# Casts on VectorE, k evacuation on ScalarE and hand-made instruction orders in an attention and spectral-mix kernel

## The chip, the cores and the metric

The kernel runs on one core of a Trainium2 chip. The metric is the device time of one execution, in microseconds (us). An execution more than 1.5% above the fastest of its kernel counts as slow and is left out of the ratios. TensorE, VectorE, ScalarE and GpSimd are the compute engines; the profile calls them PE, DVE, ACT and POOL. PEld is TensorE's weight load. In this kernel TensorE's products go into tiles in PSUM, and nearly all else lies in tiles in SBUF. To evacuate is to copy a product out of PSUM. The granted clock is the share of TensorE's full clock that it was given.

## The reference, cut to what matters

```python
# q, k, v: (8, 8, 576, 64) float32; window 128, causal, ALiBi bias per head
scores = where((rel >= 0) & (rel < 128), q @ k.T / 8 + slope[h] * -|rel|, -1e9)
x = (softmax(scores) @ v)            # -> (8, 576, 512)

X = rfft(x, axis=1)[:, :64]          # 64 modes, complex
Y = einsum("bmd,mde->bme", X, w_r + 1j * w_i)    # 2 x 64 weights of 512 x 512, 134 MB
y = irfft(Y, n=576, axis=1)
u = x + y
out = u + relu(u @ w_ch)
```

## The kernel before

It has three stages. **Attention** works in 16 units, each being one batch and half of its heads. **The mode stage** streams 128 weight matrices of 1 MB each through TensorE. **The last stage** makes 36 output tiles. In the first stage the order of each engine's instructions is fixed by hand; in the timelines below VectorE takes its instructions in that order.

In attention the loaded q, k and v are cast from float32 to bfloat16, q and k are transposed on TensorE into PSUM (`tp`) and evacuated to SBUF (`qkT`), scores are exponentiated on ScalarE and masked on VectorE, and `values` multiplies by v and scales on VectorE into `x`. Once per batch, that is every second unit, `spectrum` multiplies `x` by a Fourier table `F`.

```python
    def casts(self, u, eng=None):
        qr, kr, vr = self.loaded.pop(u)
        ...
        for dst, src in ((qc, qr), (kc, kr)):
            (eng or nc.gpsimd).tensor_copy(dst.rearrange("p j e d -> p e j d"), src)
        vb = self.vb[u % 3]
        nc.gpsimd.tensor_copy(vb[:, :FULL, :, :D], vr[:, :FULL])
        nc.gpsimd.tensor_copy(vb[:TAIL, FULL, :, :D], vr[:TAIL, FULL])

    def transposes(self, u, w):          # w = 0: q, w = 1: k
        ...                              # nine TensorE transposes into the one PSUM tile tp
        if w == 0:
            nc.scalar.copy(dst, src)
        else:
            nc.scalar.copy(dst[:, 0], src[:, 0])
            nc.vector.tensor_copy(dst[:, 1], src[:, 1])

    def scores(self, u, kt):
        ...                              # matmuls into sc, exp on ScalarE into att
        for c0, m0, n in ...:
            nc.vector.tensor_tensor(out=heads[...], in0=heads[...], in1=mask[...], op=ALU.mult)

    def spectrum(self, b):
        xt = self.ps.tile([P, 4, 2, NM], FP32, tag="tp")     # the same PSUM buffer as tp
        ...                                                  # 20 matmuls with F
        nc.scalar.copy(view[:, :, 8 + b : 24 : 8, :], xt)
        nc.vector.tensor_scalar_mul(view[:, :, b, :], xt[:, :, 1, :], -1.0)
        if b % 2:
            nc.gpsimd.tensor_copy(self.x[:64, b, FULL], self.x[:64, b - 1, FULL])

    for u in range(n + 1):
        ...
        at.casts(u + 1)
        at.scores(u, 0); at.scores(u, 1)
        at.values(u - 1, 0)
        at.transposes(u + 1, 0)
        at.scores(u, 2); at.scores(u, 3)
        at.values(u - 1, 1)
        at.transposes(u + 1, 1)
        if u > 0 and u % at.NG == 0:
            at.spectrum(u // at.NG - 1)
```

A tile of the last stage, whose order a scheduler decides:

```python
        def finish(i):
            mm = ps.tile([P, DM], FP32, tag="acc")
            nc.tensor.matmul(mm, lhsT=ident, rhs=XW[:, i], start=True, stop=False)
            inverse(mm, 0, bs, st, False)
            nc.scalar.activation(r, mm, AF.Relu)
            yy = ps.tile([P, DM], FP32, tag="my", bufs=3)
            pool_adds = i % 2 == 1
            if pool_adds:
                nc.gpsimd.tensor_tensor(out=r, in0=r, in1=x, op=ALU.add)
            else:
                nc.tensor.matmul(yy, lhsT=ident, rhs=x, start=True, stop=False)
            inverse(yy, 1, bs, st, pool_adds)
            nc.vector.tensor_tensor(out=o, in0=yy, in1=r, op=ALU.add)
            ...                              # store by DMA
```

The softmax here doesn't subtract the row's maximum and nothing guards it: scores larger than these inputs give would overflow.

## Time and profile before

The median of three runs is 561.41 us (559.18 to 564.18), and 561.64 with a fourth; the profiled execution is another one. The profiled execution has three stages, whose borders are the first and the last matmul with the mode weights:

| stage | from, us | to, us | length, us |
|---|---|---|---|
| attention (with setup) | 0 | 199.0 | 199.0 |
| mode stage | 199.0 | 509.9 | 310.9 |
| last stage | 509.9 | 562.0 | 52.1 |

The head of the profile page: the span, each engine's busy time with its share of the span, and the busy tenths of GpSimd in 40 slices of 14 us.

```profile
span 562.0 us, 6337 instructions
PE 359.8 (64%) x2406; PEld 186.4 (33%) x2406; DVE 212.2 (38%) x328; ACT 162.6 (29%) x230; POOL 94.8 (17%) x124
...
POOL 6732163145150000000000000000000000000453
```

GpSimd works only in attention (the first 12 slices) and in the last stage. The table by windows gives each engine's busy us (and its instructions) in each stage, then the granted clock, the DMA share and the bandwidth.

```profile
20.00:199.00 179.00, 99.86 (x1322) 77.74 (x1318) 123.17 (x181) 90.09 (x102) 58.79 (x68) 0.71 0.62 182
199.00:509.00 310.00, 216.05 (x893) 90.94 (x894) 45.78 (x87) 39.05 (x69) 0.00 (x0) 0.78 0.98 406
509.00:562.00 53.00, 40.70 (x171) 15.48 (x168) 30.21 (x46) 26.42 (x45) 20.80 (x18) 0.85 0.52 179
```

The columns after the window's length are PE, PEld, DVE, ACT and POOL. In attention no engine is full (VectorE 123 of 179 us). The mode stage is bound by DMA (0.98 busy). In the last stage TensorE is busiest.

The groups of instructions show the masks (two groups, one for each buffer) and one small copy of the Fourier table: busy time, then the mean of one in ns, then idle time before them and its releaser.

```profile
L229 DVE TENSOR_TENSOR att_134<-att_134,mask 128x1024 bf16<-128x1024 bf16 (+2 forms) x40 | 42.7, 1099 | 9.4 <-ACT att_134 L223 9.4
L229 DVE TENSOR_TENSOR att_133<-att_133,mask 128x1024 bf16<-128x1024 bf16 (+2 forms) x40 | 33.8, 867 | 22.5 <-ACT att_133 L223 22.5
...
L74 DVE COPY F<-F 64x128 bf16<-64x128 bf16 x1 | 6.1, 6073 | 0.7 <-ACT F L41 0.7
```

The masks take 76.5 us together. The median of one is 0.69 us, yet the longest takes 7.11 us. The timeline shows why (start, duration, engine, instruction, and in brackets the idle time before it with its releaser):

```profile
88.98 4.62 DVE L229 TENSOR_TENSOR att_133<-att_133,mask 128x1024 bf16<-128x1024 bf16 x3 [0.97 <-ACT att_133 L223]
93.76 0.82 DVE L267 TENSOR_TENSOR x<-av,rec 128x640 bf16<-128x640 f32 x1
94.50 0.75 DVE L203 COPY qkT_132<-tp 128x576 bf16<-128x576 bf16 x1
95.30 2.29 PE L281 MATMUL xt<-F,x 128*128 128x128 bf16 x20 [5.87 <-DVE qkT_132 L203]
...
116.60 1.14 POOL L185 CAST qc<-qr 128x1152 bf16<-128x1152 f32 x1
117.61 5.88 DVE L229 TENSOR_TENSOR att_134<-att_134,mask 128x1024 bf16<-128x1024 bf16 x2 [0.56 <-ACT att_134 L223]
117.69 1.14 POOL L185 CAST kc<-kr 128x1152 bf16<-128x1152 f32 x1
...
121.20 1.14 POOL L185 CAST kc<-kr 128x1152 bf16<-128x1152 f32 x1
```

Two masks that should take 1.4 us take 5.88 us, while six GpSimd casts run back to back from 116.60 to 122.34. And at 95.30 TensorE has waited 5.87 us: `spectrum` takes the PSUM buffer of the k transposes, which is free only after VectorE's half of the k evacuation at 94.50, and this copy stands in VectorE's queue behind the long masks and a value scaling. The list of waits from 20 to 199 us adds up such holes (total us, times, longest):

```profile
PE xt L281 <- DVE qkT_132 L203: 28.4, 7, 5.9
PE av L259 <- DVE x L267: 25.5, 17, 4.9
PE sc L218 <- DVE qkT_131 L203: 11.8, 7, 4.2
```

### The profile page before, as it was taken

What the parts mean: (1) busy time and instruction counts of PE and PEld (TensorE: products, weight loads), DVE (VectorE), ACT (ScalarE), POOL (GpSimd) and SP (SyncE); (2) the same over time, 40 slices, a digit from 0 to 9 for tenths busy, and PEclk for the clock granted to TensorE, in tenths of its full rate; (3) what the DMA queues carried; (4) which work ended last, traced back from release to release, by engine and by line L of the source; (5) the groups of instructions that cost most, each with busy time, mean ns of one, the idle gap of its engine ahead of it and who ended that gap; (6) DMA issues with size and microseconds to landing.
All of it is one profiled execution on the core that took longest, in us unless ns stands there. A gap on an engine that the chain in (4) does not pass through costs nothing.

```text
span 562.0 us, 6337 instructions
## 1 busy us (share of the span) xinstructions
PE 359.8 (64%) x2406; PEld 186.4 (33%) x2406; DVE 212.2 (38%) x328; ACT 162.6 (29%) x230; POOL 94.8 (17%) x124
## 2 busy tenths in 40 slices
PE   1355555644645676757865765757675867657994
PEld 1244444543434532322322322323332322222331
DVE  5776676686677550110111011231011001002674
ACT  4454544744654321100110110221110100002573
POOL 6732163145150000000000000000000000000453
PEclk9976766776766678688679867898976866685999
DMA  9998469669550059999999999998999999990476
GB/s 256 298 280 285 119 189 274 193 158 295 165 188 2 2 233 426 421 419 422 423 421 420 422 420 423 422 419 306 424 420 423 420 419 422 422 411 27 159 275 223
DMA packets 71087, 173.44 MB, mean 309 GB/s; under 512 B 41360, under 2 KB 41360, under 8 KB 54672
## 3 DMA queue, kind: packets, MB, share of 16 engines
q1 hardware_dynamic: 71056, 173.03, 82.3%
q8 instruction: 19, 0.31, 0.2%
q14 instruction: 12, 0.10, 0.1%
HBM read 163.58 MB, written 9.44 MB: 308 GB/s over the span
## 4 chain that ended last, share of the span: by engine, by line
DMA 44%; PE 23%; DVE 19%; ACT 9%; issue 2%; POOL 1%; SPq 0%; POOLq 0%; ACTq 0%; DVEq 0%
DMA w<-in_moe_w_i_dram 43%; PE acc L409 6%; DVE att_134 L229 6%; PE sc L218 3%; DVE att_133 L229 3%; PE av L259 3%; ACT att_133 L223 3%; DVE x L267 3%; ACT att_134 L223 2%; PE xt L281 2%; PE tp L196 2%; PE zz L438 2%; PE mm L465 1%; DVE Zs L446 1%; ACT r L485 1%
## 5 line engine op out<-in xcount | busy, mean ns | idle before, releaser
L409 PE MATMUL acc<-w,XC 128*32 128x512 bf16 x512 | 144.7, 459 | 53.9 <-DMA w<-in_moe_w_i_dram 30.1
L409 PEld LDWEIGHTS <-XC 128*32 128x32 bf16 x512 | 56.4, 142 | 123.8 <-issue 104.7
L489 POOL TENSOR_TENSOR r<-r,x 128x512 f32<-128x512 f32 x18 | 20.8, 1155 | 338.4 <-ACT r L485 337.6
L418 DVE CAST yq<-acc 128x512 bf16<-128x512 f32 x16 | 11.1, 692 | 168.1 <-PE acc L409 168.1
L465 PE MATMUL mm<-wch,xT 128*128 128x512 bf16 x144 | 48.8, 474 | 5.3 <-DVE xT L462 5.2
L229 DVE TENSOR_TENSOR att_134<-att_134,mask 128x1024 bf16<-128x1024 bf16 (+2 forms) x40 | 42.7, 1099 | 9.4 <-ACT att_134 L223 9.4
L467 ACT CAST XW<-mm 128x512 bf16<-128x512 f32 x36 | 21.1, 585 | 78.2 <-PE mm L465 78.2
L462 DVE COPY xT<-tr 128x512 bf16<-128x512 bf16 x36 | 15.3, 425 | 72.2 <-PE tr L460 72.2
L229 DVE TENSOR_TENSOR att_133<-att_133,mask 128x1024 bf16<-128x1024 bf16 (+2 forms) x40 | 33.8, 867 | 22.5 <-ACT att_133 L223 22.5
L223 ACT ACTIVATE att_133<-sc 128x1024 bf16<-128x1024 f32 x32 | 31.1, 1027 | 23.3 <-PE sc L218 23.3
L427 ACT COPY YT<-tr 128x128 bf16<-128x128 bf16 x8 | 5.8, 728 | 99.6 <-DVE YT L427 99.6
L281 PE MATMUL xt<-F,x 128*128 128x128 bf16 x160 | 15.4, 277 | 29.5 <-DVE qkT_132 L203 28.4
L218 PE MATMUL sc<-qkT_131 64*128 64x256 bf16 (+2 forms) x160 | 16.9, 343 | 26.8 <-DVE qkT_131 L203 18.0
L223 ACT ACTIVATE att_134<-sc 128x1024 bf16<-128x1024 f32 x32 | 31.1, 1028 | 2.5 <-PE sc L218 2.4
L460 PE MATMUL tr<-ident,x 128*128 128x128 bf16 x144 | 18.4, 268 | 18.8 <-ACT YT L430 12.5
L430 ACT COPY YT<-tr 128x64 bf16<-128x64 bf16 x16 | 5.8, 530 | 82.3 <-DVE YT L430 82.3
L494 DVE TENSOR_TENSOR o<-yy,r 128x512 f32<-128x512 f32 x36 | 23.6, 687 | 13.5 <-POOL r L489 6.8
L267 DVE TENSOR_TENSOR x<-av,rec 128x640 bf16<-128x640 f32 x32 | 26.4, 825 | 1.1
L460 PEld LDWEIGHTS <-x 128*128 128x128 bf16 x144 | 14.6, 123 | 30.5 <-issue 19.2
L485 ACT ACTIVATE r<-mm 128x512 f32<-128x512 f32 x36 | 21.3, 596 | 10.9 <-DVE o L494 5.9
L465 PEld LDWEIGHTS <-xT 128*128 128x128 bf16 x144 | 13.0, 110 | 34.4 <-DVE xT L462 20.9
L281 PEld LDWEIGHTS <-x 128*128 128x128 bf16 x160 | 14.3, 134 | 30.2 <-DVE x L267 26.4
(101 smaller groups left out, 441.1 us busy)
## 6 DMA issues: line engine op xcount, KB each, us to landing
w<-in_moe_w_r_dram SPq DMA_DIRECT2D x64, 1024.0 KB, 15.8
w<-in_moe_w_i_dram SPq DMA_DIRECT2D x64, 1024.0 KB, 17.5
qr<-in_q_dram SPq DMA_DIRECT2D x16, 576.0 KB, 4.6
kr<-in_k_dram SPq DMA_DIRECT2D x16, 576.0 KB, 5.6
vr<-in_v_dram SPq DMA_DIRECT2D x64, 128.0 KB, 4.9
out_dram<-o SPq DMA_DIRECT2D x32, 256.0 KB, 2.1
vr<-in_v_dram SPq DMA_DIRECT2D x16, 64.0 KB, 4.5
w<-in_moe_w_ch_dram SPq DMA_DIRECT2D x1, 1024.0 KB, 5.8
```

Source lines behind the costliest of these rows:

```text
L218: nc.tensor.matmul(sc[:, e, h * 256 + c0 : h * 256 + c0 + n], lhsT=qkT[row, 1, h, k0 : k0 + P], rhs=qkT[row, 0, h, q0 : q0 + n],)
L223: nc.scalar.activation(att, sc.rearrange("p e n -> p (e n)"), AF.Exp, scale=1.0 / math.sqrt(D))
L229: nc.vector.tensor_tensor(out=heads[:, :, c0 : c0 + n], in0=heads[:, :, c0 : c0 + n], in1=mask[:, :, m0 : m0 + n], op=ALU.mult,)
L267: nc.vector.tensor_tensor(out=self.x[:, b, :, cs].rearrange("p t (h d) -> p h t d", h=2), in0=tiles[:, :, :, :D], in1=rec.unsqueeze(-1).br ...
L281: nc.tensor.matmul(xt[:, a].rearrange("p r m -> p (r m)"), lhsT=self.x[:, b, st, a::4], rhs=self.F[:, st + (b % 2 if st == FULL else 0)], ...
L409: nc.tensor.matmul(acc[32 * j : 32 * j + 32], lhsT=XC[:, c0 : c0 + 31 * NM + 1 : NM], rhs=w[:, a].bitcast(BF16)[:, 1::2], start=(ri == 0 a ...
L460: nc.tensor.transpose(tr[:, dt], x[:, dt * P : (dt + 1) * P], ident)
L465: nc.tensor.matmul(mm, lhsT=xT[:, dt], rhs=wch[:, dt], start=(dt == 0), stop=(dt == 3))
L467: nc.scalar.copy(XW[:, i], mm)
L485: nc.scalar.activation(r, mm, AF.Relu)
L489: nc.gpsimd.tensor_tensor(out=r, in0=r, in1=x, op=ALU.add)
L494: nc.vector.tensor_tensor(out=o, in0=yy, in1=r, op=ALU.add)
```

## The change

The intent is to keep GpSimd out of attention, to take the evacuation of q and k off VectorE, and to lay the work of each unit out by hand so that no engine's queue waits behind another. Four parts can be told apart:

1. The casts of q, k and v and a small copy of `x` move from GpSimd to VectorE.
2. The whole k evacuation, and the scaling by −1 in the spectrum, move to ScalarE.
3. The order in attention is written out piece by piece; masks are separated from their scores, and the spectrum runs one iteration later. The setup and the first unit are reordered too.
4. The last stage gets its own PSUM pool (three banks for `mm`, three for `yy`, two for `zz`), an order by hand, and identity products that start two tiles ahead. The tiles of a pair of batches are also taken in another order, and `o` gets a fifth buffer.

```diff
-            (eng or nc.gpsimd).tensor_copy(dst.rearrange("p j e d -> p e j d"), src)
-        nc.gpsimd.tensor_copy(vb[:, :FULL, :, :D], vr[:, :FULL])
-        nc.gpsimd.tensor_copy(vb[:TAIL, FULL, :, :D], vr[:TAIL, FULL])
+        nc.vector.tensor_copy(dst.rearrange("p j e d -> p e j d"), self.loaded[u]["qk".index(w)])
+            nc.vector.tensor_copy(vb[:, :FULL, :, :D], vr[:, :FULL])
+            nc.vector.tensor_copy(vb[:TAIL, FULL, :, :D], vr[:TAIL, FULL])
 ...
-        if w == 0:
-            nc.scalar.copy(dst, src)
-        else:
-            nc.scalar.copy(dst[:, 0], src[:, 0])
-            nc.vector.tensor_copy(dst[:, 1], src[:, 1])
+        nc.scalar.copy(
+            dst.rearrange("q h (p j) -> q h p j", j=TPP),
+            tp.rearrange("q j (h p) -> q h p j", h=2),
+        )
 ...
-        nc.vector.tensor_scalar_mul(view[:, :, b, :], xt[:, :, 1, :], -1.0)
+        nc.scalar.mul(view[:, :, b, :], xt[:, :, 1, :], -1.0)
 ...   # the order of one unit, conditions cut
+            at.cast(u + 1, "q")
+            at.scores(u, 0); at.scores(u, 1); at.masked(u, 0)
+            at.values(u - 1, 0)
+            at.spectrum((u - 3) // 2)            # odd u
+            at.transpose(u + 1, "q")
+            at.masked(u, 1)
+            at.cast(u + 1, "k")
+            at.scores(u, 2)
+            at.transpose(u + 1, "k")
+            at.masked(u, 2); at.scores(u, 3)
+            at.values(u - 1, 1)
+            at.masked(u, 3)
+            at.cast(u + 1, "v")
 ...   # the last stage
+        ps = mctx.enter_context(tc.tile_pool(name="tps", bufs=3, space=PSUM, reuse_waits="tile"))
+        mctx.enter_context(tc.manual_schedule(engines=ALL))
+        def begin(i):
+            mm = ps.tile([P, DM], FP32, tag="mm", name="mm")
+            yy = ps.tile([P, DM], FP32, tag="yy", name="yy")
+            nc.tensor.matmul(mm, lhsT=ident, rhs=XW[:, i], start=True, stop=False)
+            if not pool_adds(i):
+                nc.tensor.matmul(yy, lhsT=ident, rhs=tiles[i][0], start=True, stop=False)
+        begin(0)
+        begin(1)
+        for i in range(len(tiles)):
+            done = end(i)                        # both inverse products, relu, GpSimd's add
+            begin(i + 2)
+            if pending is not None:
+                store(i - 1, *pending)
```

More of the change, by code (lines that the diff above doesn't have):

```diff
@@ L131, in __init__ @@
         self.att = [fix.tile([P, FULL * 8 * P + 64], BF16, name=f"att{i}") for i in range(2)]
-        self.loaded, self.cast = {}, {}
+        self.loaded, self.casted = {}, {}
     def fixtures(self):
@@ L176, in load, with cast, transpose @@
         self.loaded[u] = qr, kr, vr
-    def casts(self, u, eng=None):
+    def cast(self, u, w):
         nc = self.nc
-        qr, kr, vr = self.loaded.pop(u)
-        qc = self.mid.tile([P, TPP, 2, D], BF16, tag="qc")
-        kc = self.mid.tile([P, TPP, 2, D], BF16, tag="kc")
-        for dst, src in ((qc, qr), (kc, kr)):
-            (eng or nc.gpsimd).tensor_copy(dst.rearrange("p j e d -> p e j d"), src)
-        vb = self.vb[u % 3]
-        nc.gpsimd.tensor_copy(vb[:, :FULL, :, :D], vr[:, :FULL])
-        nc.gpsimd.tensor_copy(vb[:TAIL, FULL, :, :D], vr[:TAIL, FULL])
-        self.cast[u] = qc, kc
-    def transposes(self, u, w):
+        if w == "v":
+            vr, vb = self.loaded.pop(u)[2], self.vb[u % 3]
+            nc.vector.tensor_copy(vb[:, :FULL, :, :D], vr[:, :FULL])
+            nc.vector.tensor_copy(vb[:TAIL, FULL, :, :D], vr[:TAIL, FULL])
+            return
+        dst = self.mid.tile([P, TPP, 2, D], BF16, tag=w, name=w)
+        nc.vector.tensor_copy(dst.rearrange("p j e d -> p e j d"), self.loaded[u]["qk".index(w)])
+        self.casted[u, w] = dst
+    def transpose(self, u, w):
         nc = self.nc
-        src = self.cast[u][w]
+        src = self.casted.pop((u, w))
         tp = self.ps.tile([P, TPP, P], BF16, tag="tp")
@@ L196, in transposes @@
             nc.tensor.transpose(tp[:, j], src[:, j].rearrange("p e d -> p (e d)"), self.ident)
-        dst = self.qkT[u % 2][:, w, :, : self.S].rearrange("q h (p j) -> q h p j", j=TPP)
-        src = tp.rearrange("q j (h p) -> q h p j", h=2)
-        if w == 0:
-            nc.scalar.copy(dst, src)
-        else:
-            nc.scalar.copy(dst[:, 0], src[:, 0])
-            nc.vector.tensor_copy(dst[:, 1], src[:, 1])
+        dst = self.qkT[u % 2][:, "qk".index(w), :, : self.S]
+        nc.scalar.copy(
+            dst.rearrange("q h (p j) -> q h p j", j=TPP),
+            tp.rearrange("q j (h p) -> q h p j", h=2),
+        )
     def scores(self, u, kt):
@@ L225, in scores, with masked @@
         )
+    def masked(self, u, kt):
+        nc = self.nc
+        g = self.units[u][1]
+        att = self.att[u % 2][:, kt * 8 * P : (kt + 1) * 8 * P]
         heads = att.rearrange("p (h n) -> p h n", h=4)
@@ L288, in spectrum @@
         nc.scalar.copy(view[:, :, 8 + b : 24 : 8, :], xt)
-        nc.vector.tensor_scalar_mul(view[:, :, b, :], xt[:, :, 1, :], -1.0)
+        nc.scalar.mul(view[:, :, b, :], xt[:, :, 1, :], -1.0)
         if b % 2:
-            nc.gpsimd.tensor_copy(self.x[:64, b, FULL], self.x[:64, b - 1, FULL])
+            nc.vector.tensor_copy(self.x[:64, b, FULL], self.x[:64, b - 1, FULL])
 @with_exitstack
@@ L320 @@
     wch = const.tile([P, 4, DM], BF16, name="wch")
-    with tc.tile_pool(name="setup", bufs=1) as pool, tc.manual_schedule(engines=ALL):
+    ordered = ExitStack()
+    ordered.enter_context(tc.manual_schedule(engines=ALL))
+    with tc.tile_pool(name="setup", bufs=1) as pool:
         make_identity(nc, ident)
@@ L349 @@
         at = _Attention(tc, actx, q, k, v, (ident, F, ek), x, XC)
-        actx.enter_context(tc.manual_schedule(engines=ALL))
         n = len(at.units)
@@ L355 @@
         at.masks(0)
-        at.casts(0, nc.vector)
-        at.transposes(0, 0)
-        at.transposes(0, 1)
         at.masks(4)
         nc.gpsimd.memset(XC[:, 4 * NC * NM :], 0.0)
+        for w in "qk":
+            at.cast(0, w)
+            at.transpose(0, w)
+        at.cast(0, "v")
         for u in range(n + 1):
+            now, nxt, old = u < n, u + 1 < n, u > 0
             if u + 2 < n:
                 at.load(u + 2)
-            if u < n and (u % 2 == 1 or u == n - 2):
+            if now and (u % 2 == 1 or u == n - 2):
                 load_w()
-            if u + 1 < n:
-                at.casts(u + 1)
-            for kt in (0, 1):
-                if u < n:
-                    at.scores(u, kt)
-            if u > 0:
-                at.values(u - 1, 0)
-            if u + 1 < n:
-                at.transposes(u + 1, 0)
-            for kt in (2, 3):
-                if u < n:
-                    at.scores(u, kt)
-            if u > 0:
+            if nxt:
+                at.cast(u + 1, "q")
+            if now:
+                at.scores(u, 0)
+                at.scores(u, 1)
+                at.masked(u, 0)
+            if old:
+                at.values(u - 1, 0)
+            if u > 2 and u % 2 == 1:
+                at.spectrum((u - 3) // 2)
+            if nxt:
+                at.transpose(u + 1, "q")
+            if now:
+                at.masked(u, 1)
+            if nxt:
+                at.cast(u + 1, "k")
+            if now:
+                at.scores(u, 2)
+            if nxt:
+                at.transpose(u + 1, "k")
+            if now:
+                at.masked(u, 2)
+                at.scores(u, 3)
+            if old:
                 at.values(u - 1, 1)
-            if u + 1 < n:
-                at.transposes(u + 1, 1)
-            if u > 0 and u % at.NG == 0:
-                at.spectrum(u // at.NG - 1)
+            if now:
+                at.masked(u, 3)
+            if nxt:
+                at.cast(u + 1, "v")
             if u == 12:
                 nc.gpsimd.tensor_copy(wch, wq[0])
+        at.spectrum(B - 1)
+        ordered.close()
     with ExitStack() as mctx:
@@ L395 @@
         big = mctx.enter_context(tc.tile_pool(name="xw", bufs=1))
-        ps = mctx.enter_context(tc.tile_pool(name="fps", bufs=2, space=PSUM))
+        pctx = ExitStack()
+        ps = pctx.enter_context(tc.tile_pool(name="fps", bufs=2, space=PSUM))
         XW = big.tile([P, 9 * (B // 2), DM], BF16, name="XW")
@@ L431, in modes, with spectra @@
                              src[:, :, :, par::2])
-        def spectra(hf, bp):
-            zz = ps.tile([P, 2, DM], FP32, tag="zz", bufs=1)
+        def spectra(ps, hf, bp):
+            zz = ps.tile([P, 2, DM], FP32, tag="zz", bufs=1, name="zz")
+            lhsT = [YT[:, hf, et, 2 * bp : 2 * bp + 2].rearrange("p b r m -> p (b r m)")
+                    for et in range(4)]
             for et in range(4):
-                lhsT = YT[:, hf, et, 2 * bp : 2 * bp + 2].rearrange("p b r m -> p (b r m)")
-                nc.tensor.matmul(zz[:, 0], lhsT=lhsT, rhs=wch[:, et],
+                nc.tensor.matmul(zz[:, 0], lhsT=lhsT[et], rhs=wch[:, et],
                                  start=(et == 0), stop=(et == 3))
-                nc.tensor.matmul(zz[:, 1, et * P : (et + 1) * P], lhsT=lhsT, rhs=ident,
+            for et in range(4):
+                nc.tensor.matmul(zz[:, 1, et * P : (et + 1) * P], lhsT=lhsT[et], rhs=ident,
                                  start=True, stop=True)
+            yield
             for i in range(2):
@@ L446, in spectra @@
                 nc.vector.tensor_copy(Zs[row, b, 1], zz[row, 1])
+                yield
         tiles = []
         for bp in range(B // 2):
-            for st in range(FULL):
-                for bb in range(2):
+            for bb in range(2):
+                for st in range(FULL):
                     tiles.append((x[:, 2 * bp + bb, st], [2 * bp + bb], st))
@@ L455, in project @@
         def project(i):
-            x = tiles[i][0]
+            xi = tiles[i][0]
             tr = ps.tile([P, 4, P], BF16, tag="tr", bufs=1)
             for dt in range(4):
-                nc.tensor.transpose(tr[:, dt], x[:, dt * P : (dt + 1) * P], ident)
+                nc.tensor.transpose(tr[:, dt], xi[:, dt * P : (dt + 1) * P], ident)
             xT = pool.tile([P, 4, P], BF16, tag="xT")
@@ L467, in project, with pool_adds @@
             nc.scalar.copy(XW[:, i], mm)
+        todo = 0
+        for g in range(NM // 4):
+            modes(g)
+            if 8 <= g < 12:
+                for _ in spectra(ps, 0, g - 8):
+                    pass
+            for i in range(todo, min(todo + 3, len(tiles))):
+                project(i)
+                todo = i + 1
+        pctx.close()
+        ps = mctx.enter_context(
+            tc.tile_pool(name="tps", bufs=3, space=PSUM, reuse_waits="tile")
+        )
+        mctx.enter_context(tc.manual_schedule(engines=ALL))
+        open_tiles = {}
+        def pool_adds(i):
+            return i % 2 == 1
+        def begin(i):
+            if i >= len(tiles):
+                return
+            mm = ps.tile([P, DM], FP32, tag="mm", name="mm")
[3 more added lines that the diff above has]
+                nc.tensor.matmul(yy, lhsT=ident, rhs=tiles[i][0], start=True, stop=False)
+            open_tiles[i] = mm, yy
         def inverse(dst, part, bs, st, start):
@@ L477, in inverse, with end @@
                 )
-        def finish(i):
-            x, bs, st = tiles[i]
-            mm = ps.tile([P, DM], FP32, tag="acc")
-            nc.tensor.matmul(mm, lhsT=ident, rhs=XW[:, i], start=True, stop=False)
+        def end(i):
+            xi, bs, st = tiles[i]
+            mm, yy = open_tiles.pop(i)
             inverse(mm, 0, bs, st, False)
@@ L485, in finish, with store @@
             nc.scalar.activation(r, mm, AF.Relu)
-            yy = ps.tile([P, DM], FP32, tag="my", bufs=3)
-            pool_adds = i % 2 == 1
-            if pool_adds:
-                nc.gpsimd.tensor_tensor(out=r, in0=r, in1=x, op=ALU.add)
-            else:
-                nc.tensor.matmul(yy, lhsT=ident, rhs=x, start=True, stop=False)
-            inverse(yy, 1, bs, st, pool_adds)
-            o = pool.tile([P, DM], FP32, tag="o", bufs=4)
+            inverse(yy, 1, bs, st, pool_adds(i))
+            if pool_adds(i):
+                nc.gpsimd.tensor_tensor(out=r, in0=r, in1=xi, op=ALU.add)
+            return r, yy
+        def store(i, r, yy):
+            xi, bs, st = tiles[i]
+            o = pool.tile([P, DM], FP32, tag="o", bufs=5)
             nc.vector.tensor_tensor(out=o, in0=yy, in1=r, op=ALU.add)
@@ L500, in finish @@
                     nc.sync.dma_start(out=out[b, FULL * P :, :], in_=o[row])
-        todo = 0
-        for g in range(NM // 4):
-            modes(g)
-            if 8 <= g < 12:
-                spectra(0, g - 8)
-            for i in range(todo, min(todo + 3, len(tiles))):
-                project(i)
-                todo = i + 1
-        spectra(1, 0)
-        for bp in range(B // 2):
-            if bp + 1 < B // 2:
-                spectra(1, bp + 1)
-            for i in range(9 * bp, 9 * bp + 9):
-                finish(i)
+        begin(0)
+        begin(1)
+        for _ in spectra(ps, 1, 0):
+            pass
+        pending, steps = None, iter(())
+        for i in range(len(tiles)):
[3 more added lines that the diff above has]
+                store(i - 1, *pending)
+            pending = done
+            if i % 9 == 2 and i // 9 + 1 < B // 2:
+                steps = spectra(ps, 1, i // 9 + 1)
+            next(steps, None)
+        store(len(tiles) - 1, *pending)
 _INS = ['q', 'k', 'v', 'moe_w_r', 'moe_w_i', 'moe_w_ch']
```

## The prediction

> **What bounds it now.** The windows view shows three stages. Attention, 0 to 199 us: no engine is full (VectorE about 0.7 busy, ScalarE 0.5, TensorE 0.55). The chain of waits there hops between VectorE masks, TensorE and ScalarE; two units (one batch, with one spectrum) take 22.2 us, the mean spacing of the spectrum matmuls between 49.7 and 182.8 us. The mode stage, 199 to 508 us: it streams weights at 421 GB/s with the DMA engines full, and 43% of the chain is one weight load. The last stage, 508 to 562 us: TensorE over 0.9 busy, 36 tiles in about 41 us.
>
> **A hidden cost.** A mask multiply takes 0.69 us (median), yet single ones take up to 7.1 us, and in the timeline these lie beside GpSimd casts (117.6 us: two masks take 5.9 us while casts run back to back). The Trainium skill ("GPSIMD Engine Reference", Specifications) says that GpSimd shares VectorE's SBUF interfaces, with contention for VectorE instructions with two SBUF inputs or in a 2-port mode; the trace agrees. Masks total 76.5 us; at their undisturbed lengths it would be about 45. One 64x128 copy of the Fourier table takes 6.07 us beside GpSimd casts, and first scores wait for it.
>
> **The change, costed.** Per unit VectorE gains two casts (0.76 us each on VectorE in this trace) and the v casts (estimate 0.9, from that rate) and loses half of the k evacuation (0.75); masks lose about 2 us of stretching. Its busy time hardly moves, but stretches vanish. ScalarE gains 0.5 us per unit (1.12 against 0.65).
>
> Estimate of the new cycle without a spectrum: VectorE from one value scaling to the k cast (1.08 + 0.76 + 0.9 + 0.76 + 0.72 + 1.08 + 0.72 + 0.76 = 6.8), then k transposes (1.0), scores (0.7), values (1.1): 9.7 us. With a spectrum, spectrum and both transposes pass one after another through one PSUM buffer with ScalarE emptying it: about 11.0. So 20.7 per two units instead of 22.2: 10 us over the stage. The start gains about 5 (short table copy), first units, fewer stretches and the tail the rest: the mode stage starts near 179 us instead of 199.
>
> Mode stage: same loads at the same rate, 309 us, unchanged within 3.
>
> Last stage: hand order starts the identity products two tiles ahead and runs spectra one block ahead. But odd tiles keep one PSUM bank for their second sum, so each waits for the store two tiles before it: 0.41 (product to relu) + 0.60 + 1.16 (GpSimd add) + 0.69, with gaps 3.0 us, plus 1.3 of TensorE work, per four tiles: 1.09 us per tile against 1.14 now. With spectra on top: no gain, 0 to 3 us lost; I count +2.
>
> **Predicted**: 543 us (range 530 to 556). Faster by over 2%: 0.76; within 2%: 0.21; slower: 0.03.
>
> **Right or wrong, by step.** Mask multiplies all near 0.69 us; table copy under 0.5; GpSimd under 30 us busy; two units 20 to 21.5 us apart; first mode matmul at 172 to 186 us; mode stage 306 to 312 us long; last stage 50 to 58 us, its chain showing GpSimd adds.
>
> **What would make it wrong.** TensorE's granted clock (0.66 to 0.77 in attention) may fall as it is used more, lengthening the cycle. Loads need about 8 us of DMA time per unit (share of DMA in the windows): little slack if units get shorter than I think. ScalarE may be the real limit (6.7 us per unit of work in a fixed order). The tile order may take TensorE off its limit in the last stage, giving up to 8 us more; or its waits may cost 10.

## The result and the profile after

The median of four runs is 525.44 us (521.79 to 528.08), against 561.64 us for the kernel before in the same rounds. The ratio is 0.9351, with a 95% interval of 0.9279 to 0.9422: faster by 6.5%, below the low end of the predicted range. A ratio here is the mean time of one kernel's fast runs over that of the other's of the same rounds, so it is not quite the ratio of the medians. The changed kernel was run again later beside experiments (e14_after): 524.44 us, ratio 0.9330 [0.9297, 0.9364].

| stage | before, us | predicted | after, us |
|---|---|---|---|
| first mode matmul (end of attention) | 199.0 | 179 (172 to 186) | 159.7 |
| mode stage, length | 310.9 | 309 | 308.8 |
| last stage, length | 52.1 | 54 (50 to 58) | 57.9 |
| two units of attention, with one spectrum | 22.2 | 20.7 | 17.7 |

The head of the page and the windows of the changed kernel:

```profile
span 526.4 us, 6272 instructions
PE 351.9 (67%) x2389; PEld 179.8 (34%) x2406; DVE 193.3 (37%) x370; ACT 172.9 (33%) x238; POOL 34.0 (6%) x58
...
POOL 7010000000000000000000000000000000002443
```

```profile
20.00:160.00 140.00, 97.16 (x1289) 69.36 (x1286) 106.13 (x217) 94.73 (x105) 3.38 (x10) 0.77 0.77 233
160.00:468.00 308.00, 207.38 (x879) 89.80 (x890) 45.75 (x87) 39.04 (x69) 0.00 (x0) 0.78 0.99 409
468.00:526.00 58.00, 40.40 (x168) 15.82 (x170) 30.41 (x46) 26.16 (x45) 20.78 (x18) 0.88 0.47 164
```

VectorE took over all the casts and is still busy 17 us less in attention (106.13 against 123.17), while GpSimd is nearly idle there (3.38 us). Busy time counts overlapping records once. What left VectorE is the evacuation of k (11.2 us before) and the scaling of the spectrum (3.4 us), and the masks shrank:

```profile
L231 DVE TENSOR_TENSOR att_132<-att_132,mask 128x1024 bf16<-128x1024 bf16 (+2 forms) x40 | 23.2, 598 | 6.9 <-ACT att_132 L220 6.7
L231 DVE TENSOR_TENSOR att_133<-att_133,mask 128x1024 bf16<-128x1024 bf16 (+2 forms) x40 | 22.4, 578 | 10.2 <-ACT att_133 L220 9.9
```

The masks fell from 76.5 to 45.7 us, the longest from 7.11 to 1.48 us. The timeline shows the table copy of the start, a stretch of VectorE's queue in attention, and two moments of the last stage:

```profile
6.80 0.23 DVE L74 COPY F<-F 64x128 bf16<-64x128 bf16 x1 [0.73 <-ACT F L41]
...
106.30 0.68 DVE L231 TENSOR_TENSOR att_132<-att_132,mask 128x1024 bf16<-128x1024 bf16 x1
106.89 0.75 DVE L187 CAST k<-kr 128x1152 bf16<-128x1152 f32 x1
107.69 0.69 DVE L231 TENSOR_TENSOR att_132<-att_132,mask 128x1024 bf16<-128x1024 bf16 x1
...
497.24 1.16 POOL L540 TENSOR_TENSOR r<-r,x 128x512 f32<-128x512 f32 x1 [0.99 <-ACT r L537]
497.29 0.38 PE L527 MATMUL yy<-Zs,FT 128*128 128x512 bf16 x1 [0.87 <-DVE o L546]
```

The 64x128 copy takes 0.23 us instead of 6.07. In the queue, each instruction starts about 0.6 to 0.8 us after the one before: a mask with a recorded duration of 0.68 us is followed 0.59 us later. At 497.29 the second product of an output tile waits for VectorE's store add of an earlier tile.

In attention (20 to 160 us) TensorE's waits add up to 43 us, against 78 before (20 to 199 us), and the longest holes are gone:

```profile
PE tp L195 <- ACT att_132 L220: 8.6, 5, 1.9
PE tp L195 <- DVE k L187: 7.3, 5, 2.7
PE tp L195 <- DVE q L187: 7.2, 8, 1.0
```

The list of waits for the last stage, of the changed kernel and then of the kernel before:

```profile
DVE o L546 <- POOL r L540: 13.2, 16, 1.8
PE yy L527 <- DVE o L546: 8.3, 12, 1.2
...
DVE o L494 <- POOL r L489: 6.8, 11, 1.1
PE yy L491 <- DVE o L494: 1.2, 3, 0.6
PE yy L474 <- DVE o L494: 0.7, 1, 0.7
```

L474 is the second product of an output tile before, as L527 is after; L491 is its identity product.

So the gain of the profiled executions is 39.3 us in attention and 2.1 us in the mode stage, less 5.8 us lost in the last stage: 562.0 − 39.3 − 2.1 + 5.8 = 526.4. Of the 39.3 us, 9.1 lie before the first spectrum (49.7 against 40.6 us), 26.8 in the six full intervals between spectra, and 3.4 after the seventh spectrum.

### The profile page after: what moved, and what is told of

It reads as the page before. It is cut to its first block, busy times and chain, and to the rows that moved or that the text cites. A ratio compares the mean times of both kernels' runs of the same rounds, so it can differ in the third digit from the quotient of the medians.

```text
span 526.4 us, 6272 instructions
## 1 busy us (share of the span) xinstructions
PE 351.9 (67%) x2389; PEld 179.8 (34%) x2406; DVE 193.3 (37%) x370; ACT 172.9 (33%) x238; POOL 34.0 (6%) x58
## 4 chain that ended last, share of the span: by engine, by line
DMA 47%; PE 25%; DVE 11%; ACT 7%; issue 5%; SPq 3%; POOL 2%; POOLq 0%; DVEq 0%; ACTq 0%
DMA w<-in_moe_w_i_dram 46%; PE acc L428 6%; PE av L261 4%; PE tp L195 3%; PE sc L215 2%; SPq L172 2%; PE zz L458 2%; ACT att_133 L220 2%; PE xt L283 2%; POOL r L540 2%; DVE att_133 L231 1%; DVE Zs L468 1%; PE mm L488 1%; ACT Zs L467 1%; DVE x L269 1%
## 5 line engine op out<-in xcount | busy, mean ns | idle before, releaser
L428 PE MATMUL acc<-w,XC 128*32 128x512 bf16 x512 | 140.8, 453 | 56.5 <-DMA w<-in_moe_w_i_dram 32.5
L488 PE MATMUL mm<-wch,xT 128*128 128x512 bf16 x133 | 44.9, 465 | 9.1 <-DVE xT L485 8.4
L540 POOL TENSOR_TENSOR r<-r,x 128x512 f32<-128x512 f32 x18 | 20.8, 1154 | 342.9 <-ACT r L537 341.6
L220 ACT ACTIVATE att_132<-sc 128x1024 bf16<-128x1024 f32 x32 | 32.1, 1033 | 0.3
L220 ACT ACTIVATE att_133<-sc 128x1024 bf16<-128x1024 f32 x32 | 31.9, 1029 | 0.5
L195 PE MATMUL tp<-ident,k 128*128 128x128 bf16 x144 | 15.8, 282 | 22.4 <-DVE k L187 9.0
L546 DVE TENSOR_TENSOR o<-yy,r 128x512 f32<-128x512 f32 x36 | 23.6, 687 | 13.5 <-POOL r L540 13.2
L195 PE MATMUL tp<-ident,q 128*128 128x128 bf16 x144 | 12.7, 243 | 21.0 <-DVE q L187 15.2
L231 DVE TENSOR_TENSOR att_133<-att_133,mask 128x1024 bf16<-128x1024 bf16 (+2 forms) x40 | 22.4, 578 | 10.2 <-ACT att_133 L220 9.9
L231 DVE TENSOR_TENSOR att_132<-att_132,mask 128x1024 bf16<-128x1024 bf16 (+2 forms) x40 | 23.2, 598 | 6.9 <-ACT att_132 L220 6.7
L483 PEld LDWEIGHTS <-x 128*128 128x128 bf16 x144 | 14.7, 123 | 30.4 <-issue 19.1
L197 ACT COPY qkT_131<-tp 128x1152 bf16<-128x1152 bf16 x16 | 17.9, 1119 | 19.6 <-PE tp L195 19.6
```

Source lines behind the costliest of these rows:

```text
L195: nc.tensor.transpose(tp[:, j], src[:, j].rearrange("p e d -> p (e d)"), self.ident)
L220: nc.scalar.activation(att, sc.rearrange("p e n -> p (e n)"), AF.Exp, scale=1.0 / math.sqrt(D))
L231: nc.vector.tensor_tensor(out=heads[:, :, c0 : c0 + n], in0=heads[:, :, c0 : c0 + n], in1=mask[:, :, m0 : m0 + n], op=ALU.mult,)
L428: nc.tensor.matmul(acc[32 * j : 32 * j + 32], lhsT=XC[:, c0 : c0 + 31 * NM + 1 : NM], rhs=w[:, a].bitcast(BF16)[:, 1::2], start=(ri == 0 a ...
L483: nc.tensor.transpose(tr[:, dt], xi[:, dt * P : (dt + 1) * P], ident)
L488: nc.tensor.matmul(mm, lhsT=xT[:, dt], rhs=wch[:, dt], start=(dt == 0), stop=(dt == 3))
```

## The experiments

The prediction missed 19 us in attention. Three explanations were open. The first: the stretched VectorE instructions are worth more than their added durations, because they stand in front of something that TensorE waits for. A rival: the evacuation on ScalarE is the larger part, because it takes VectorE out of the way from the k transposes to the next scores. Another rival: the hand-made order does it, by overlapping the spectrum. For the last stage, the theory was that PSUM banks make the product wait for the store.

Twelve kernels were run in three batches. The kernel before had medians of 563.24, 562.18 and 561.86 us in them.

### e1_dvecasts: part 1 alone, in the old order

```diff
-            (eng or nc.gpsimd).tensor_copy(dst.rearrange("p j e d -> p e j d"), src)
+            nc.vector.tensor_copy(dst.rearrange("p j e d -> p e j d"), src)
```
(the same for the two casts of v and the small copy of `x`)

> The kernel before, with one part of the change alone: all casts (and the small x copy) on VectorE, the old order and everything else kept. Theory C (contention: the attention stage gained because GpSimd casts no longer stretch VectorE instructions): first mode matmul at 165 to 175 us instead of 199, total 528 to 540, masks together near 45 us busy. Rival O (order: it gained because work was interleaved by hand): masks get short, but the 2.4 us block of casts stands in front of each unit's masks, first mode matmul at 188 to 200, total 550 to 562.

Measured: 532.85 us, ratio 0.9463 [0.9395, 0.9530]. The first mode matmul moved from 199.0 to 168.6 us. The group of all 80 masks:

```profile
L229 DVE TENSOR_TENSOR att<-att,mask 128x1024 bf16<-128x1024 bf16 (+2 forms) x80 | 43.2, 576 | 8.6 <-ACT att L223 8.3
```

The longest mask takes 0.69 us, the table copy 0.40 us. Moving the casts gives 30 us on its own, although VectorE takes on about 38 us of casts and is rid of only 35 in the masks: from 20 us to the end of attention its recorded durations add up to 131 us against 130 (busy time, with overlapping records counted once, is 117 against 123). What falls is TensorE's waiting, and no single VectorE instruction is 3 to 7 us late any more. Added over the whole stage, the listed waits of TensorE fall from 78 to 58 us.

### e8_evac: the k evacuation alone, in the old order

```diff
-            nc.scalar.copy(dst[:, 0], src[:, 0])
-            nc.vector.tensor_copy(dst[:, 1], src[:, 1])
+            nc.scalar.copy(dst, src)
```

> The kernel before, with one part alone: the whole k evacuation on ScalarE; casts on GpSimd and the old order kept. Theory E (the second cause: half of the k evacuation stood last in VectorE's queue, behind stretched masks, and TensorE waited for it 28 us before spectra and 13 us before scores): first mode matmul at 178 to 190 us, total 542 to 554. If contention is all: the masks are as stretched as before (70 us or more in all) and the stage ends at 195 to 200, total 558 or more.

Measured: 542.67 us, ratio 0.9672 [0.9613, 0.9731]; first mode matmul at 178.0 us, 21 us earlier. The masks are as long as before (74.2 us, the longest 7.11). The waits of TensorE:

```profile
PE av L258 <- DVE x L266: 27.8, 19, 5.5
PE xt L280 <- DVE x L266: 22.6, 8, 5.0
PE sc L217 <- ACT qkT L202: 11.0, 8, 1.7
```

The next scores wait for ScalarE now, at most 1.7 us at a time, where VectorE's half held them up to 4.2 us. The spectrum still waits for VectorE's value scaling. Of the 21 us, 11.8 are in TensorE's listed waits (77.6 to 65.8) and 8 in its busy time (99.9 to 91.9, at a granted clock of 0.75 against 0.71). The second is an observation; whether the clock rose because of the new pattern was not tested.

### e10_castevac: both, in the old order

The two edits above together.

> The kernel before with casts on VectorE and the k evacuation on ScalarE, in the old order. If the order still counts when both are done: first mode matmul at 162 to 169 us (after: 156 to 160), total 525 to 533. If the order counts for nothing then: 156 to 161 us, total 517 to 522 with the old last stage.

Measured: 523.40 us, ratio 0.9325 [0.9261, 0.9389]; first mode matmul at 159.8 us; masks 44.5 us. This is the length of attention in the changed kernel's profile to 0.1 us, without its hand-made order. The total is not to be set beside the changed kernel's, because the last stage here is the old one; e4_oldlast, with the same last stage and the new attention, took 518.13 us in another batch. So with the other two parts in place the order adds some 5 us to the median gain (in these profiles 159.8 against 155.7 us to the first mode matmul; against the changed kernel's own 159.7 it adds nothing).

### e9_order: the order alone, with casts on GpSimd and half of k on VectorE

The changed kernel with parts 1 and 2 undone, except the scaling by −1.

> The kernel after with two parts undone: casts on GpSimd and half of the k evacuation on VectorE, so that of the attention changes the order alone is left. If the order is a cause of its own: first mode matmul at 172 to 184 us, total 535 to 548. If the order gains only through the evacuation: 190 us or later, total 555 or more.

Measured: 543.54 us median, one of four runs slow; ratio of fast runs 0.9657 [0.9580, 0.9735]; first mode matmul at 173.1 us; masks 62.1 us, the longest 3.67 us. Taken alone, the order is worth 26 us in attention. The masks are stretched about as often (11 of the 80 above 1.2 us, against 12 before) but less far (the longest 3.67 us against 7.11). Whether that or the place of the stretched masks makes the gain was not separated.

### e2_poolcasts: the changed kernel with its casts on GpSimd

```diff
-        nc.vector.tensor_copy(dst.rearrange("p j e d -> p e j d"), self.loaded[u]["qk".index(w)])
+        eng = nc.gpsimd if u else nc.vector
+        eng.tensor_copy(dst.rearrange("p j e d -> p e j d"), self.loaded[u]["qk".index(w)])
```
(and the casts of v and the copy of `x`)

> The kernel after, with one part undone: the casts of all later units back on GpSimd, at the places of the new order. Theory C: masks are stretched again (over 60 us in all), first mode matmul at 180 to 195 us, total 545 to 560. Rival O: at most a few us lost, first mode matmul at 158 to 168 us, total 523 to 533.

Measured: two fast runs (526.37 and 531.60 us) and two slow ones (540.16 and 536.87); ratio of fast runs 0.9389 [0.9303, 0.9475]. The slow ones are slow by their time alone: their granted clocks (0.799 and 0.792) are like those of the fast ones (0.804 and 0.793). The profile fell on the slowest run, so its stages are not compared with others; the two fast runs lie 1 and 6 us above the changed kernel's median, and the mean of all four about 9 us above its mean. The loss of 20 us that the first explanation expected did not show. With the new order and the evacuation on ScalarE, putting the casts back on GpSimd thus costs less than the 20 us that it costs in the old order (e8_evac against e10_castevac), but two fast runs are few and no fast profile shows why. What the profile does show is one instruction:

```profile
101.48 1.14 POOL L188 CAST k<-kr 128x1152 bf16<-128x1152 f32 x1
...
104.25 5.93 DVE L232 TENSOR_TENSOR att<-att,mask 128x1024 bf16<-128x1024 bf16 x1 [3.20 <-ACT att L221]
...
108.50 1.14 POOL L188 CAST k<-kr 128x1152 bf16<-128x1152 f32 x1
```

A single mask starts inside a run of nine casts that follow one another without a gap, and ends 0.54 us after the last of them (108.50 + 1.14 = 109.64; 104.25 + 5.93 = 110.18). The casts keep their 1.14 us. The Trainium skill ("SBUF — State Buffer", section "SBUF: two separate sides") calls the port pair of VectorE and GpSimd an exclusive lock, held for a whole instruction, with the loser fully blocked. The trace agrees and shows more: this mask was not let in between two casts. The fast profile of the kernel before has such masks too, and one that was let in:

```profile
21.93 0.85 POOL L188 CAST vb_130<-vr 64x256 bf16<-64x256 f32 x1
22.74 1.60 POOL L185 CAST qc<-qr 128x1152 bf16<-128x1152 f32 x1
...
161.84 7.71 DVE L229 TENSOR_TENSOR att_134<-att_134,mask 128x1024 bf16<-128x1024 bf16 x2 [0.56 <-ACT att_134 L223]
```

The first of the two masks from 161.84 takes 7.11 us and ends 0.54 us after the last of seven casts that follow one another without a gap. But a mask that starts at 21.04 ends at 22.53, while the casts go on, and the small cast beside it takes 0.85 us in place of 0.39. So a mask can be kept out through a run of casts, but is not always; what decides it was not found.

### e5_twice: the changed kernel with a second, useless copy of each cast on GpSimd

```diff
+            nc.gpsimd.tensor_copy(
+                self.spare.rearrange("p (j e d) -> p e j d", j=TPP, e=2),
+                self.loaded[u]["qk".index(w)])
```
(and the same for v; nobody reads `spare`)

> The kernel after, with the suspected cost added and nothing else: GpSimd makes every cast a second time into a tile that nobody reads. No instruction waits for it, save that a raw buffer is free only when both have read it. Theory C: VectorE masks and casts stretch again, first mode matmul moves from 160 to 175 us or later, total 540 or more. Rival O: nothing moves by more than 3 us, total 523 to 530.

Measured: 542.12 us, ratio 0.9625 [0.9560, 0.9689], 17 us over the changed kernel; first mode matmul at 174.1 us, 14 us later. VectorE's busy time in attention is 123.9 us against 106.1: masks 58.3 us in place of 45.7, and the k casts 0.96 us each in place of 0.75. The longest mask takes 1.62 us only. In this timeline the GpSimd casts wait for loads and come mostly singly or in twos, so that VectorE is held by one at a time. GpSimd work that nothing depends on thus costs about its stretching of VectorE. One confound stays: these copies also hold the load buffers longer.

### e3_halfk: the changed kernel with half of k on VectorE

```diff
-        nc.scalar.copy(dst, src)                     # q and k
+        if w == "q":
+            nc.scalar.copy(dst, src)
+        else:
+            nc.scalar.copy(dst[:, 0], src[:, 0])
+            nc.vector.tensor_copy(dst[:, 1], src[:, 1])
```

> The kernel after with half of the k evacuation back on VectorE. With GpSimd idle nothing is stretched, and the half takes 0.75 us more of VectorE and 0.47 less of ScalarE per unit. Cycle theory (VectorE's work from one value scaling to the k cast is on the cycle, but the evacuation comes after it): at most 0.5 us per unit, first mode matmul at 158 to 168 us, total 523 to 533. Theory E, if it held without stretching too: 170 us or later, total 536 or more.

Measured: 542.61 us, ratio 0.9665 [0.9612, 0.9718]; first mode matmul at 175.8 us, 16 us later than in the changed kernel, where the cycle estimate allowed for 7 at most. The masks are not stretched (45.3 us). The timeline of VectorE:

```profile
114.59 0.75 DVE L187 CAST k<-kr 128x1152 bf16<-128x1152 f32 x1
117.31 0.76 DVE L203 COPY qkT<-tp 128x576 bf16<-128x576 bf16 x1 [1.96 <-ACT qkT L202]
117.98 0.68 DVE L234 TENSOR_TENSOR att<-att,mask 128x1024 bf16<-128x1024 bf16 x1
```

After the k cast VectorE has nothing it may do until TensorE has transposed k and ScalarE has copied its half; in the changed kernel the next mask follows the k cast after 0.8 us (106.89 to 107.69). Such waits add up to 36.4 us, 2.6 us in each of 14 units. Against the changed kernel VectorE is busy 7.5 us more (113.6 against 106.1, from 20 us to the end of attention) and waits 8.1 us more (40.9 against 32.8). That these sum to about the 16 us says little, since busy time and waits fill the stage on any engine; it is the timeline that shows VectorE standing in front of this copy. The granted clock was only 0.60 in this profile's attention, against 0.77; but two more runs with a mean clock of 0.862 and 0.864 over the whole kernel took 542.75 and 545.17 us, no shorter, which speaks against a low clock as the cause. Their attention was not profiled.

### e7_spec4: the changed kernel with 4 of the 20 spectrum matmuls

```diff
-            for st in range(FULL + 1):
+            for st in range(1):
...
-                    start=(st == 0), stop=(st == FULL),
+                    start=True, stop=True,
```
The result is wrong (relative error 0.021).

> The kernel after with 4 of the 20 matmuls of each spectrum (wrong result on purpose). The prediction put units with a spectrum on the chain spectrum, evacuation, q transposes, evacuation, k transposes through one PSUM buffer: then each of the seven spectra inside the loop saves about 1 us and the last one 1.9, the mode stage starts 7 to 11 us earlier, total 514 to 519. If VectorE's cycle is the limit in those units too, only the last spectrum shows: 1 to 3 us earlier, total 521 to 524.

Measured: 522.04 us, ratio 0.9273 [0.9226, 0.9320], 2.4 us below e14_after. The last three full intervals between spectra are 17.0 to 17.1 us in both kernels, and all six are 17.3 us in the mean against 17.7. Of the 4.4 us by which the mode stage starts earlier, about half lie in those six intervals and half after the seventh spectrum, where less work is left to overlap the last one. Even the first half need not come from the edit: e6_banks, with all 20 matmuls, has six intervals of 17.1 us. So in the changed kernel the spectrum's matmuls run beside other waits and cost almost nothing in the middle of the stage.

### e4_oldlast: the new attention with the old mode and last stages

The code after attention is that of the kernel before.

> The kernel after, with the mode stage and the last stage of the kernel before. If the hand order of the last stage costs what the traces show (57.9 us from the last mode matmul to the end, against 52.1 before), the total is 519 to 521, below both kernels. If that difference came from the shorter attention stage (clock, state of the chip) and not from the order, the last stage stays at 57 to 58 us and the total at 525.

Measured: 518.13 us, ratio 0.9193 [0.9140, 0.9247]. Its last stage takes 52.4 us against 57.9 and 54.0 in the two profiles of the changed kernel, so the new last stage loses time. The 6 to 7 us between the medians are not all of it, however: in this profile attention, whose code is the same, ends at 155.7 us instead of 159.7.

### e6_banks: the new last stage with four banks for `yy` and two for `mm`

```diff
-            mm = ps.tile([P, DM], FP32, tag="mm", name="mm")
-            yy = ps.tile([P, DM], FP32, tag="yy", name="yy")
+            mm = ps.tile([P, DM], FP32, tag="mm", name="mm", bufs=2)
+            yy = ps.tile([P, DM], FP32, tag="yy", name="yy", bufs=4)
...
-        begin(1)
-            begin(i + 2)
+            begin(i + 1)
```

> The kernel after; in the last stage four PSUM banks for the second sum and two for the first instead of three and three, and tiles begun one ahead instead of two, so that odd tiles have two banks of their own. If odd tiles wait for the store two tiles before because they share one bank (TensorE waits 8.3 us for those stores in the trace of after), the waits vanish, the last stage takes 48 to 53 us instead of 57.9, total 515 to 521. Rival (the order of the tiles, or the spectra in one block, costs the time): the waits move elsewhere, the last stage stays at 56 us or more, total 523 to 527.

Measured: 517.58 us, one of six runs slow, ratio of fast runs 0.9184 [0.9141, 0.9228], against 0.9330 for e14_after on the same chip. The last stage takes 51 us. The wait of VectorE for GpSimd's add in its last stage, half of the 13.2 us above:

```profile
DVE o L546 <- POOL r L540: 6.5, 14, 1.4
```

TensorE's wait for the store add is gone from the list (8.3 us in the changed kernel), and TensorE is busy 9.3 and 9.4 of 10 us in the middle of the stage (485 to 505 us), against 8.2 and 7.7, at a granted clock of 1.00 in both. In the built program of the change, the second sum of every odd tile but the last uses the same one of the three banks, so it waits for the store two tiles earlier, which comes late because it waits for GpSimd's add. With four banks the odd tiles take turns in two. The Trainium skill ("Perfetto Trace Analysis", section "Optimizing Tensor Performance") asks for independent matmul groups to rotate through different banks so that evacuation overlaps the next group; this pair of runs agrees, with 8.3 us of waits at stake. The edit also starts tiles one ahead instead of two, so banks and distance were not tried apart.

### e13_banks_r4: e6_banks with one more buffer for `r` and one less for `o`

```diff
-            r = pool.tile([P, DM], FP32, tag="r", bufs=3)
+            r = pool.tile([P, DM], FP32, tag="r", bufs=4)
...
-            o = pool.tile([P, DM], FP32, tag="o", bufs=5)
+            o = pool.tile([P, DM], FP32, tag="o", bufs=4)
```

> As e6_banks, with four buffers for the relu result and four for the output (three and five there). If ScalarE waits for a free relu buffer once the banks are free, the last stage is 1 to 3 us shorter than in e6_banks; if TensorE is the limit by then, no difference beyond 1 us.

Measured: 517.00 us, ratio 0.9198 [0.9166, 0.9230]: the same total as e6_banks within the interval. The last stage of its profile takes 48.3 us against 50.8 in e6_banks, the 1 to 3 us less that were expected if the buffer of `r` limits; but the granted clock there is 0.95 against 0.84, and attention is 4.1 us longer. Whether the buffer limits stays open.

### e14_after: the changed kernel again, as the yardstick of the last batch

> The kernel after, unchanged, on this chip beside the others: the yardstick for the last stage and for the run to run spread of the attention stage. First mode matmul at 155 to 161 us, last stage 57 to 59 us, total 521 to 528.

Measured: 524.44 us, ratio 0.9330 [0.9297, 0.9364]. Attention ends at 159.6 us as in the first profile; the last stage takes 54 us instead of 57.9, at a higher granted clock, with the same 8.2 us of TensorE's wait for the store. Single profiles of the last stage thus scatter by some 4 us, and attention by as much: the same attention code ended at 155.6 in e6_banks and at 159.7 in e13_banks_r4. Yet the two profiles of the changed kernel agree in attention to 0.1 us; whether its length is chance or belongs to each kernel is open. Taking the mean of the fast runs, e6_banks is 8.2 us below e14_after. Between the two profiles 3.2 of 8.0 us lie in the last stage and 4.0 in attention; e13_banks_r4, whose attention is as long as here, has a last stage 5.7 us shorter. So the banks are worth 3 to 6 us in the last stage by the profiles.

### All together

| casts | k evacuation | order | run | first mode matmul, us | total, us |
|---|---|---|---|---|---|
| GpSimd | half VectorE | old | before | 199.0 | 561.64 |
| VectorE | half VectorE | old | e1_dvecasts | 168.6 | 532.85 |
| GpSimd | ScalarE | old | e8_evac | 178.0 | 542.67 |
| VectorE | ScalarE | old | e10_castevac | 159.8 | 523.40 |
| GpSimd | half VectorE | new | e9_order | 173.1 | 543.54 |
| VectorE | half VectorE | new | e3_halfk | 175.8 | 542.61 |
| GpSimd | ScalarE | new | e2_poolcasts | slow profile | 526.37 and 531.60 (fast runs) |
| VectorE | ScalarE | new | after | 159.7 | 525.44 |

In the old order the casts alone gain 30 us, the evacuation alone 21, both 39 and not 51. The lists of waits fit an overlap, each removing one of two factors of one wait: the stretched mask that makes VectorE late, and the copy on VectorE's late queue that TensorE needs. TensorE's waits for that copy add up to 41.7 us before, 22.6 in e1_dvecasts and none in e8_evac, where the spectrum waits 22.6 us for the value scaling instead. In the new order the balance shifts: the evacuation is worth 16 us (e3_halfk) and the casts 1 to 6 (fast runs of e2_poolcasts; about 9 by the mean of all four); with half of k on VectorE the casts are worth nothing there (e9_order and e3_halfk within 1 us). Of the three explanations, the first two hold together, each able to stand in for much of the other; the third, the order, is a substitute for them rather than an addition. The new last stage adds to the totals of all rows with the new order: 54.0 to 57.9 us in six fast profiles, against 52.1 to 52.9 in five with the old one, about 3 us in the mean.

## Why the prediction was right or wrong

**Direction and mechanism: right.** The stretching of VectorE beside GpSimd casts was real and went away as predicted: masks 45.7 us (predicted about 45), table copy 0.23 us (under 0.5), the first mask 5.9 us earlier (15.11 against 21.04 us; about 5 was predicted for the start). The setup was reordered as well, so the 5.9 us need not all come from the table copy. e1_dvecasts and e5_twice show it from both sides. GpSimd was busy 34.0 us where "under 30" was predicted; 20.8 of these are the last stage's adds.

**Mode stage: right.** 308.8 us against 309.

**Last stage: right in mechanism, and about right in size.** The bank argument was predicted, with +2 us; the first profile has +5.8 and the second +2 us against the kernel before, and the six fast profiles with the new last stage lie about 3 us above the five with the old one. The medians differ by more (6 to 7 us from e4_oldlast, 8 from e6_banks), but about 4 us of that lie in attention in the profiles. From the first to the last store add a tile takes 1.29 and 1.22 us in the two profiles, against 1.15 before; the 1.09 us of the estimate left the spectra out. The runs show that the banks (with the distance of the starts) are the cause, not how the excess divides.

**The step that failed: the new cycle.** It was estimated at 9.7 us for a unit without a spectrum and "about 11.0" with one, 20.7 for two; measured were 8.95 and 8.92 us in the mean from one k cast to the next, and spectra 17.7 us apart. (Where a unit is taken to begin shifts the two means by up to half a microsecond; the pair stays.) Over seven pairs that is 3.0 × 7 = 21 us, more than the whole miss of 17.6. Two terms of the sum were mis-sized, and one effect was left out of it:

- *The spectrum unit, about 2 us each, 14 us in all.* The prediction put the spectrum and both transposes in a row through one PSUM buffer. e7_spec4 takes away 16 of 20 matmuls and the spacing falls by 0.4 us only: in the new order the spectrum's matmuls hide behind other waits. Its evacuation was not taken away in any run.
- *The VectorE block of 6.8 us.* It was a sum of eight recorded durations. From start to start it takes 6.1 to 6.3 us, because each recorded duration overlaps the next by about 0.1 us. That accounts for most of the 0.75 us that a unit without a spectrum is shorter.
- *The k evacuation.* It was booked as busy time alone: 0.75 us less for VectorE, 0.5 us more for ScalarE. e8_evac shows 21 us for it in the old order, e3_halfk 16 us in the new one. Its cost is not its length: TensorE waits until VectorE comes to it, or VectorE stands still in front of it.

The last also fits the direction of the error: an engine's share of busy time (VectorE 0.7) was used as the measure of what a move is worth, when the gain lies in what waits behind it.

**What would make it wrong.** The clock did not fall (0.77 in attention's window, 0.71 before), the loads kept up: the DMA share is 0.77 and no load stands among the longer waits of TensorE or VectorE in attention. ScalarE was busy 94.7 of 140 us, which in a fixed order does not clear it as a limit; no run tried that.

**Left open.** How e9_order gains 26 us with the casts still on GpSimd, and why the new order seems to bear GpSimd's casts better (e2_poolcasts, two fast runs); how the evacuation's 21 us divide between shorter waits and the higher clock that went with them; whether e6_banks owes its gain to four banks or to starting tiles one ahead; and why the same attention code ends at 155.6 us in some kernels and at 159.7 in others.

The best version measured is the new attention with four `yy` banks (e6_banks 517.58, e13_banks_r4 517.00), which beats the kernel before by 8% and the changed kernel by about 1.5%. The old last stage does as well (e4_oldlast 518.13).

## What to carry to other kernels

Before costing a move by its busy time, look in the timeline at what stands behind the instruction in its engine's queue and who waits for that: moving a 0.75 us copy was worth 21 us here (e8_evac). When the same instruction has a median of 0.7 us and a maximum of 7, look for GpSimd work beside it. Recorded durations of VectorE overlap (a mask of 0.68 us is followed 0.59 us later), so cycle times should be read from start to start, and two remedies for one wait don't add up, so try each alone and both together.

## What the Trainium skill lacked or had wrong

- "SBUF — State Buffer" (section "SBUF: two separate sides") says that the port pair is locked for one whole instruction. It lacks what happens when GpSimd instructions follow one another without a gap: a waiting VectorE instruction can be kept out to the end of the run (a 0.69 us mask took 7.11 us in the kernel before), or be let in while the casts go on (1.49 us at 21.04 us, same profile). With casts that came singly or in twos the longest mask was 1.62 us (e5_twice).
- "GPSIMD Engine Reference" (section "Specifications") names the contention without a size; here 80 masks took 76.5 us beside GpSimd casts and 43 to 46 us without. Its figure of 1.96 times (section "Performance versus the Vector engine") is for an elementwise add; a time for casts is not in that table, and here the q and k casts took 1.14 us on GpSimd and 0.75 on VectorE, a ratio of 1.5.
